# Reading wo in long runs inside the passes, and keeping four slabs of w1 in their buffers through one turn of a decode kernel

## The chip, the cores and the metric

One core of one Trainium2 chip. Times are device microseconds of one execution. Unless said otherwise a number "before" or "after" for a whole kernel is the median of several executions, and a number from inside a kernel is from the one execution that was profiled.

## The reference, cut to what matters

Two layers of attention for one new token over a cache of 65536 positions, each followed by a dense part with squared ReLU; the same caches and weights serve both layers. The function returns the result and the gradients of all inputs.

```python
def _A_ref(x, k_cache, v_cache, wq, wo):        # 32 query heads, 4 kv heads, 65536 positions, 128 wide
    q = (x @ wq) ...                            # wq 1024 x 4096
    p = softmax(q @ k * 128 ** -0.5)
    return (p @ v).reshape(1, 1, 4096) @ wo     # wo 4096 x 1024
def _B_ref(x, w1, b1, w2, b2):                  # w1 1024 x 3584, w2 3584 x 1024
    h = x @ w1 + b1
    return relu(h) ** 2 @ w2 + b2
x = x + _A_ref(ln(x), ...); x = x + _B_ref(ln(x), ...)
x = x + _A_ref(ln(x), ...); x = x + _B_ref(ln(x), ...)
# outputs: x, and jax.vjp of it at grad_out: dx, dK, dV, dwq, dwo, dw1, db1, dw2, db2; all bf16
```

## The kernel before

The kernel runs four passes over the caches: two forward ones, then two backward ones. Between two passes lies a "turn" with the dense parts. Everything large goes through one arena of slots of 8 KB per partition. In a pass, the rest of the work (the products with wq and wo, and in the fourth pass the weight gradients) is cut into steps by Python generators, and the pipeline takes at most one background step per item.

How a weight is cut into slabs, and how wo and w1 are read:

```python
def slabs(name, load, nk, kper, ncols, ahead=1, flat=False):
    def fetch():                       # two adjoining slots if there are any: one load of 2 MB; else 1 MB each
        ...
        if ks and flat and NOW["wide"] and not odd_one():
            i = take_pair()
        ...
        nc.sync.dma_start(out=v, in_=load(k, kn))
def wo_slabs(g, ahead=1):
    v = A_wo.rearrange("(kc p) n -> p kc n", p=P)      # a partition's piece of a row block: 2048 bytes
    return slabs("s_wo", lambda k, kn: v[:, g * R + k:g * R + k + kn, :], R, 4, 1024, ahead, True)
def w1_slabs(ahead=1):
    v = rows_of(B_w1)                                  # 7168 bytes per partition and slab, eight slabs
    return slabs("s_w1", lambda k, kn: v[:, k:k + kn, :], DC, 1, F, ahead)
```

The product with wo in a forward pass (`g_wo`) and the one that gives dO in a backward pass (`g_dO`), with the end of the latter:

```python
def g_wo(L, xacc, g, ps=ps_bg, it=None):
    def fin(p):
        nc.vector.tensor_tensor(out=xacc[:], in0=xacc[:], in1=p, op=ALU.add)
    yield from g_mv(it or wo_slabs(g)[0], R, 8, lambda kc: L["oTb"][:, g * R + kc:g * R + kc + 1], ps, fin)

def dO_finish(L, g):
    def fin(y):
        ...                 # two DVE operations
        yield
        ...                 # one matmul
        yield
        ...                 # five small DVE operations
    return fin

def g_dO(L, dx, g):         # reads wo_slabs(g), multiplies each slab by dx broadcast, sums on ACT into y, then fin(y)
    yield from g_rowdots(wo_slabs(g)[0], R, dx[:], DC, dO_finish(L, g), "%s_dO%d" % (L["name"], g))
```

What an item of the pipeline does in the background. `urgent` holds the products of a head group, `normal` the weight gradients:

```python
class Background:
    def step(self, i):
        while self.later and i >= self.later[0][0]:
            self.add(*self.later.popleft()[1:])
        while self.urgent:
            r = next(self.urgent[0][1], "end")
            if r == "end":
                self.urgent.popleft()
                continue
            if r == "wait":
                break
            return
        while self.normal and self.done < self.total * i / self.steps:
            if next(self.normal[0], "end") == "end":
                self.normal.popleft()
            else:
                self.done += 1
                return
# fourth pass: 256 items plus 7 of lag; bg.steps = len(ITEMS[3]) - 4 = 252; bg.total = 150
```

The turn between the second and the third pass, where w1 is read twice, once for the forward product of layer 4 and once for its gradient:

```python
rows.add(w1_slabs()[0], DC, FC, lambda: dh4[:], fin_dx3, cols=f_cols, mix=True)     # second product
rows.add(wo_slabs(firstg[2])[0], R, DC, lambda: dx3[:], dO_finish(L3, firstg[2]), inplace=True)
run(g_w1(L4, ps_mv, pre=rows.fill))                                                 # first product
nc.vector.scalar_tensor_tensor(out=dh4[:], in0=dg4[:], scalar=2.0, in1=L4["r"][:], op0=ALU.mult, op1=ALU.mult)
rows.run()
```

## Time and profile before

| | before |
|---|---|
| median of three runs | 2010.06 us (2008.94 to 2014.95) |
| profiled run | 2017.21 us, clock 0.898, its span 2015.4 us |
| PE, DVE, ACT busy | 80%, 58%, 52% |
| moved | 794.97 MB in 110845 packets, mean 394 GB/s |
| last copy of scores in pass 1; in pass 2 | 351.3; 736.0 us |
| layer norm of the turn done; last ds of pass 3 | 766.2; 1148.4 us |
| first, 57th and last (64th) X of pass 4 | 1219.4; 1902.9; 1980.2 us |
| end | 2015.4 us |

The last rows are marks that I read off the records of single instructions. "ds" is the gradient of the scores in the third pass (32 of them), "dx3" the gradient that the turn hands to the third pass, and "X" the DVE product of the gradient of the probabilities (in ps_sc) and the kept exponentials E in the fourth pass, one for every four items, 64 in all. The profiled run was 2 to 8 us slower than the three others, so differences of a few microseconds between single traces are not to be trusted. The lines of the profile that carry the argument stand in the prediction.

### The profile page before, as it was taken

To read this page: it belongs to the slowest core of one execution; us is meant where nothing else is said; L and a number is where in the kernel's file an instruction comes from. 1 tells how busy PE (TensorE), PEld (TensorE's weight loads), DVE (VectorE), ACT (ScalarE), POOL (GpSimd) and SP (SyncE) were. 2 spreads that over 40 slices of the span, in tenths; PEclk is the share of its full clock that TensorE was granted. 3 is DMA by queue.
4 is the path that set the end of the run, shared out by engine and by line. 5 is a ranking of instruction groups with operands and counts; after the bars stand their busy time and mean duration, and the time that the engine had idled before them with its cause. 6 is when DMAs were issued, how large, how long until landed. Compare 5 with 4: busy or idle time off the path is not lost. (4 is left out here: it accounts for less than half of the span.)

```text
span 2015.4 us, 67001 instructions
## 1 busy us (share of the span) xinstructions
PE 1613.8 (80%) x30210; PEld 1315.4 (65%) x30210; DVE 1175.3 (58%) x2358; ACT 1043.6 (52%) x1613; POOL 144.4 (7%) x332
## 2 busy tenths in 40 slices
PE   6877787687887787868787888788778988698896
PEld 6877777677777686767777785455445555455554
DVE  5655455255555544535454476586658777577675
ACT  3444344253443353426354365586657677577675
POOL 0000000000000000000000001121111111121111
PEclk9999899699899997999888998799879889798888
DMA  9999999999999998999999986999999999999995
GB/s 389 420 419 420 419 422 399 391 406 419 420 417 419 420 404 316 371 420 420 418 413 417 394 305 254 363 404 424 421 405 404 408 419 399 358 405 424 416 377 236
DMA packets 110845, 794.97 MB, mean 394 GB/s; under 512 B 9424, under 2 KB 9438, under 8 KB 49374
## 3 DMA queue, kind: packets, MB, share of 16 engines
q1 hardware_dynamic: 86510, 624.99, 76.3%
q0 software_dynamic: 24048, 165.70, 19.9%
q8 instruction: 236, 3.87, 0.8%
q14 instruction: 51, 0.42, 0.1%
HBM read 624.96 MB, written 165.69 MB: 392 GB/s over the span
## 5 line engine op out<-in xcount | busy, mean ns | idle before, releaser
L153 DVE COPY kt<-ps_tr 128x1024 bf16<-128x1024 bf16 x724 | 497.7, 689 | 481.3 <-PE ps_tr L936 255.4
L150 ACT CAST arena<-ps_gg 128x1024 bf16<-128x1024 f32 x452 | 440.0, 1010 | 226.0 <-PE ps_gg L1303 169.7
L936 PE MATMUL ps_tr<-ident_b,arena 128*128 128x128 bf16 x3840 | 311.3, 226 | 55.7 <-DMA arena<-in_A_k_cache_dram 41.4
L936 PEld LDWEIGHTS <-arena 128*128 128x128 bf16 x3840 | 235.2, 101 | 62.3 <-DMA arena<-in_A_k_cache_dram 44.4
L153 DVE CAST arena<-ps_gg 128x1024 bf16<-128x1024 f32 (+1 forms) x191 | 228.9, 1199 | 77.3 <-PE ps_gg L1303 43.6
L150 ACT COPY kt<-ps_tr 128x1024 bf16<-128x1024 bf16 x164 | 172.3, 1055 | 185.9 <-PE ps_tr L1128 125.7
L1303 PE MATMUL ps_gg<-GG,xt 64*128 64x512 bf16 x1024 | 214.1, 417 | 46.3 <-DVE arena L153 26.1
L1038 PE MATMUL ps_acc<-arena 128*128 128x64 bf16 (+4 forms) x4096 | 204.7, 195 | 49.4 <-DMA arena<-in_A_v_cache_dram 28.9
L1249 PE MATMUL ps_tr<-ident_b,arena 128*128 128x128 bf16 x1824 | 178.2, 236 | 39.7 <-DMA arena<-in_A_v_cache_dram 38.8
L954 PE MATMUL ps_sc<-L_qpad,kt 128*128 128x64 bf16 (+7 forms) x3584 | 183.9, 194 | 19.6 <-issue 12.3
L1019 ACT ACTIVATE arena<-S_sb,L_negm 128x128 bf16<-128x128 f32 x256 | 165.7, 1003 | 58.2 <-DVE L_negm L1004 58.2
L1128 PE MATMUL ps_tr<-ident_b,arena 128*128 128x128 bf16 x1920 | 155.8, 227 | 46.5 <-DMA arena<-in_A_v_cache_dram 45.2
L1038 PEld LDWEIGHTS <-arena 128*128 128x128 bf16 x4096 | 158.5, 100 | 52.6 <-DMA arena<-in_A_v_cache_dram 32.9
L1249 PEld LDWEIGHTS <-arena 128*128 128x128 bf16 x1824 | 121.1, 105 | 94.3 <-issue 51.0
L954 PEld LDWEIGHTS <-kt 128*128 128x128 bf16 x3584 | 153.7, 100 | 25.7 <-issue 15.3
L1128 PEld LDWEIGHTS <-arena 128*128 128x128 bf16 x1920 | 118.1, 102 | 50.0 <-DMA arena<-in_A_v_cache_dram 47.9
L1329 PE MATMUL ps_acc<-X,arena 128*128 128x64 bf16 (+3 forms) x2048 | 120.7, 199 | 23.0 <-DMA arena<-in_A_k_cache_dram 23.0
L1019 ACT ACTIVATION_READ_ACCUMULATOR arena<-S_sb,L_negm 128x1 f32 x256 | 128.0, 500 | 0.0
L1329 PEld LDWEIGHTS <-arena 128*128 128x128 bf16 x2048 | 87.8, 102 | 59.4 <-issue 34.2
L1303 PEld LDWEIGHTS <-xt 64*128 64x128 bf16 x1024 | 61.2, 94 | 86.7 <-issue 48.0
L1282 PE MATMUL ps_sc<-DOB,kt 128*128 128x64 bf16 (+3 forms) x1824 | 117.7, 200 | 0.0
L1173 PE MATMUL ps_acc<-dsT,arena 128*128 128x64 bf16 (+7 forms) x2048 | 104.0, 195 | 16.7 <-DMA arena<-in_A_k_cache_dram 12.2
(269 smaller groups left out, 2129.1 us busy)
## 6 DMA issues: line engine op xcount, KB each, us to landing
arena<-in_A_k_cache_dram SPq DMA_DIRECT2D x86, 2048.0 KB, 21.4
arena<-in_A_v_cache_dram SPq DMA_DIRECT2D x83, 2048.0 KB, 21.7
out_dram<-arena POOLq DMA_DIRECT2D x151, 1024.0 KB, 11.4
arena<-in_A_v_cache_dram SPq DMA_DIRECT2D x76, 1024.0 KB, 16.2
arena<-in_A_k_cache_dram SPq DMA_DIRECT2D x76, 1024.0 KB, 14.6
arena<-in_B_w_dram SPq DMA_DIRECT2D x32, 896.0 KB, 5.9
arena<-in_A_wq_dram SPq DMA_DIRECT2D x22, 1024.0 KB, 14.3
arena<-in_A_wo_dram SPq DMA_DIRECT2D x18, 1024.0 KB, 18.5
```

The costliest lines, as they stand in the source:

```text
L150: nc.scalar.copy(out=out, in_=in_)
L153: nc.vector.tensor_copy(out=out, in_=in_)
L936: nc.tensor.transpose(pt[:, i, :], kb8[:, i, :], ident_b[:, :])
L954: nc.tensor.matmul(state["ps_s"][:, s:s + w, :].rearrange("p a b -> p (a b)"), lhsT=kt[:, i, :], rhs=L["qpad"][:, g, 0:w, :].rearrange("p ...
L1019: nc.scalar.activation(out=E(p, g, c0, SU)[:, :, h], in_=S[:, h, :], func=ACTF.Exp, bias=L["negm"][:, g, su, h:h + 1], scale=SCALE, accum_ ...
L1038: nc.tensor.matmul(ps_o[:, 0:w, :], lhsT=vb8[:, i, :], rhs=E(p, g, c, w), start=(c % SU == 0), stop=(c % SU == SU - 1), skip_group_check=True)
L1128: nc.tensor.transpose(pt[:, i, :], vb8[:, i, :], ident_b[:, :])
L1173: nc.tensor.matmul(ps_dq[:, 0:w, :].rearrange("p a b -> p (a b)"), lhsT=kb8[:, i, :], rhs=dsT[:, s:s + w, :].rearrange("p a b -> p (a b)") ...
L1249: nc.tensor.transpose(pt[:, i, :], vb8[:, i, :], ident_b[:, :])
L1282: nc.tensor.matmul(state["ps_dp"][:, s:s + w, :].rearrange("p a b -> p (a b)"), lhsT=vt[:, i, :], rhs=DOB[:, g, 0:w, :].rearrange("p a b - ...
L1303: nc.tensor.matmul(pg[:, 512 * h:512 * h + 512], lhsT=xt[64 * h:64 * h + 64, j1 // 8 + m, :], rhs=gg[64 * h:64 * h + 64, :, :].rearrange(" ...
L1329: nc.tensor.matmul(ps_dq[:, 0:w, :].rearrange("p a b -> p (a b)"), lhsT=kb8[:, i, :], rhs=X[:, s:s + w, :].rearrange("p a b -> p (a b)"), ...
```

## The change

Two intents. First, the twelve groups of wo that are read inside passes are read with eight adjoining rows per partition: 16 KB in one piece if two adjoining slots are free, else twice 8 KB, where the kernel before has pieces of 2 KB. A partition then holds other rows than before, so o is rearranged by one matmul with a 0/1 matrix before the product, and dO is rearranged back after it. Second, in the turn the first product with w1 reads slabs 4 to 7, then 0 to 3, and leaves the last four in their slots for the second product. To make room for the new constants, some small tiles shrink and the bias rows move into an arena slot.

```diff
+    def wo_runs(g):
+        v = A_wo[g * 1024:(g + 1) * 1024, :].rearrange("(p k) n -> p k n", k=8)
+        return slabs("s_wo", lambda k, kn: v[:, k:k + kn, :], R, 4, 1024, 1, True)[0]
 ...
+    def w1_twice(keep):
 ...
+        def first():
+            for k in list(range(keep, DC)) + list(range(keep)):
+                sl, w = one(k)                    # takes a slot, issues the load
+                yield k, w
+                if k < keep:
+                    kept.append((sl, w))
+                else:
+                    sl.free()
+        def again():
+            for k in range(DC):
+                sl, w = kept[k] if k < keep else one(k)
+                NOW["slab"] = sl
+                yield k, w
+                sl.free()
 ...
     def g_wo(L, xacc, g, ps=ps_bg, it=None):
 ...
+        each = ...; yield                         # one DVE operation
+        pt = ...;   yield                         # one matmul with to_runs
+        own = ...; oruns = ...; orunb = ...; yield   # three DVE operations
+        yield from g_mv(wo_runs(g), R, 8, lambda kc: orunb[:, kc:kc + 1], ps, fin)
 ...
     def g_dO(L, dx, g):
-        yield from g_rowdots(wo_slabs(g)[0], R, dx[:], DC, dO_finish(L, g), "%s_dO%d" % (L["name"], g))
+        def fin(y):
+            each = tmp.tile([P, R, 8], F32, name="run_own", bufs=1)
+            nc.vector.tensor_tensor(out=each[:, :, :], in0=y.unsqueeze(1).to_broadcast([P, R, 8]),
+                                    in1=M8[:, :].unsqueeze(2).to_broadcast([P, R, 8]), op=ALU.mult)
+            yield
+            pt = ps_mv([P, R, 8], F32)
+            nc.tensor.matmul(...)                 # with from_runs
+            yield
+            own = ...; back = ...                 # two DVE operations
+            yield
+            yield from dO_finish(L, g)(back[:, :])
+        yield from g_rowdots(wo_runs(g), R, dx[:], DC, fin, "%s_dO%d" % (L["name"], g))
 ...
+    w1a, w1b = w1_twice(4)
-    rows.add(w1_slabs()[0], DC, FC, lambda: dh4[:], fin_dx3, cols=f_cols, mix=True)
+    rows.add(w1b, DC, FC, lambda: dh4[:], fin_dx3, cols=f_cols, mix=True)
-    run(g_w1(L4, ps_mv, pre=rows.fill))
+    run(g_w1(L4, ps_mv, pre=rows.fill, it=w1a))
```

Cut: five constants, the bias rows in a slot (`rows_f`), `gmb` in one buffer, `ndt4` as 64 x 16 broadcast in the matmul, and in `g_mv` a counter for the last slab, since the slabs now come in another order.

More of the change, by code (lines that the diff above doesn't have):

```diff
@@ L126 @@
     nc.vector.tensor_tensor(out=M4x[:], in0=M8[:, 0:4], in1=M8[:, 4:8], op=ALU.add)
+    eighth = const.tile([P, 8], F32, name="eighth")
+    nc.vector.tensor_reduce(out=eighth[:], in_=ident_f[:].rearrange("p (m e) -> p e m", e=8), axis=AX.X, op=ALU.add)
+    sixt = const.tile([P, 16], F32, name="sixt")
+    nc.vector.tensor_reduce(out=sixt[:], in_=ident_f[:].rearrange("p (m e) -> p m e", e=8), axis=AX.X, op=ALU.add)
+    to_runs = const.tile([P, 8, 16], BF, name="to_runs")
+    nc.vector.tensor_copy(out=to_runs[:, :, :], in_=sixt[:, :].unsqueeze(1).to_broadcast([P, 8, 16]))
+    sixt2 = const.tile([P, 16], F32, name="sixt2")
+    nc.vector.tensor_reduce(out=sixt2[:], in_=ident_f[:].rearrange("p (a m) -> p m a", m=16), axis=AX.X, op=ALU.add)
+    from_runs = const.tile([P, 16, 8], F32, name="from_runs")
+    nc.vector.tensor_copy(out=from_runs[:, :, :], in_=sixt2[:, :].unsqueeze(2).to_broadcast([P, 16, 8]))
     load = {"act": 0.0, "dve": 0.0, "pe": 0.0}
@@ L167, in col_from_dram_f @@
         nj = n // P
-        rows = tmp.tile([nj // 4, 4 * P], BF, name="rows_f", tag="rows_f", bufs=1)
-        nc.sync.dma_start(out=rows[:], in_=v1d.rearrange("(s x) -> s x", x=4 * P))
+        sl = Slot("rows_f")
+        rows = sl.t[0:nj // 4, 0:4 * P]
+        nc.sync.dma_start(out=rows, in_=v1d.rearrange("(s x) -> s x", x=4 * P))
         pt = ps_mv([P, 4, 8], BF)
@@ L178, in col_to_dram_f @@
         nj = n // P
-        rows = tmp.tile([nj // 4, P, 4], BF, name="rows_f", tag="rows_f", bufs=1)
+        sl = Slot("rows_f", True)
+        rows = sl.t[0:nj // 4, 0:4 * P].rearrange("s (p j) -> s p j", j=4)
         c3 = col[:, :].rearrange("p (s j) -> p s j", j=4)
@@ L184, in col_to_dram_f @@
             nc.vector.tensor_copy(out=rows[:, :, j], in_=pt[:])
-        nc.gpsimd.dma_start(out=v1d.rearrange("(s x) -> s x", x=4 * P), in_=rows[:].rearrange("s p j -> s (p j)"))
+        nc.gpsimd.dma_start(out=v1d.rearrange("(s x) -> s x", x=4 * P), in_=sl.t[0:nj // 4, 0:4 * P])
+        sl.free(stored=True)
     def col_to_dram(col, n, v1d):
@@ L460, in w1_slabs, with one @@
         return slabs("s_w1", lambda k, kn: v[:, k:k + kn, :], DC, 1, F, ahead)
+    def w1_twice(keep):
+        v = rows_of(B_w1)
+        kept = []
+        def one(k):
+            sl = Slot("s_w1")
+            w = sl.t[:, 0:F]
+            nc.sync.dma_start(out=w, in_=v[:, k, :])
+            return sl, w
+        def first():
[11 more added lines that the diff above has]
+                yield k, w
+                sl.free()
+        return first(), again()
     def w2_slabs(ahead=1):
@@ L470, in g_mv @@
         first = True
+        left = nk
         for kc, slab in slab_it:
+            left -= 1
             if ps_of is ps_bg and kc % 4 == 0:
@@ L475, in g_mv @@
             for nb in range(nbk):
-                last = (kc == nk - 1) and (nb == nbk - 1)
+                last = left == 0 and nb == nbk - 1
                 nc.tensor.matmul(ps[:, nb, :], lhsT=cols(slab, nb), rhs=xcol(kc).to_broadcast([P, rep]),
@@ L868, in fin @@
             nc.vector.tensor_tensor(out=xacc[:], in0=xacc[:], in1=p, op=ALU.add)
-        yield from g_mv(it or wo_slabs(g)[0], R, 8, lambda kc: L["oTb"][:, g * R + kc:g * R + kc + 1],
-                        ps, fin)
+        if it is not None:
+            yield from g_mv(it, R, 8, lambda kc: L["oTb"][:, g * R + kc:g * R + kc + 1], ps, fin)
+            return
+        each = tmp.tile([P, R, 8], BF, name="run_each", bufs=1)
+        nc.vector.tensor_tensor(out=each[:, :, :], in0=L["oTb"][:, gsl(g)].unsqueeze(2).to_broadcast([P, R, 8]),
+                                in1=eighth[:, :].unsqueeze(1).to_broadcast([P, R, 8]), op=ALU.mult)
+        yield
+        pt = ps_mv([P, R, 8])
+        nc.tensor.matmul(pt[:, :, :].rearrange("p r k -> p (r k)"), lhsT=to_runs[:, :, :].rearrange("p a b -> p (a b)"),
+                         rhs=each[:, :, :].rearrange("p r k -> p (r k)"), start=True, stop=True)
+        yield
+        own = tmp.tile([P, 8, R], F32, name="run_own", bufs=1)
+        nc.vector.tensor_tensor(out=own[:, :, :], in0=pt[:, :, :].rearrange("p r k -> p k r"),
+                                in1=M8[:, :].unsqueeze(1).to_broadcast([P, 8, R]), op=ALU.mult)
+        oruns = tmp.tile([P, 8], F32, name="run_o")
+        nc.vector.tensor_reduce(out=oruns[:], in_=own[:, :, :], axis=AX.X, op=ALU.add)
+        orunb = tmp.tile([P, 8], BF, name="run_ob")
+        nc.vector.tensor_copy(out=orunb[:], in_=oruns[:])
+        yield
+        yield from g_mv(wo_runs(g), R, 8, lambda kc: orunb[:, kc:kc + 1], ps, fin)
     def dO_finish(L, g):
@@ L892, in g_dO @@
     def g_dO(L, dx, g):
-        yield from g_rowdots(wo_slabs(g)[0], R, dx[:], DC, dO_finish(L, g), "%s_dO%d" % (L["name"], g))
+        def fin(y):
+            each = tmp.tile([P, R, 8], F32, name="run_own", bufs=1)
+            nc.vector.tensor_tensor(out=each[:, :, :], in0=y.unsqueeze(1).to_broadcast([P, R, 8]),
+                                    in1=M8[:, :].unsqueeze(2).to_broadcast([P, R, 8]), op=ALU.mult)
+            yield
+            pt = ps_mv([P, R, 8], F32)
+            nc.tensor.matmul(pt[:, :, :].rearrange("p r k -> p (r k)"), lhsT=from_runs[:, :, :].rearrange("p a b -> p (a b)"),
+                             rhs=each[:, :, :].rearrange("p r k -> p (r k)"), start=True, stop=True)
+            yield
+            own = tmp.tile([P, R, 8], F32, name="run_own", bufs=1)
+            nc.vector.tensor_tensor(out=own[:, :, :], in0=pt[:, :, :], in1=eighth[:, :].unsqueeze(1).to_broadcast([P, R, 8]), op=ALU.mult)
+            back = tmp.tile([P, R], F32, name="run_o")
+            nc.vector.tensor_reduce(out=back[:], in_=own[:, :, :], axis=AX.X, op=ALU.add)
+            yield
+            yield from dO_finish(L, g)(back[:, :])
+        yield from g_rowdots(wo_runs(g), R, dx[:], DC, fin, "%s_dO%d" % (L["name"], g))
     def dn_finish(dn, first):
@@ L995, in low @@
                 nc.vector.tensor_reduce(out=gm[:], in_=v["ptm"][:], axis=AX.X, op=ALU.min)
-                v["gmb"] = tmp.tile([R, P], F32, name="gmb")
+                v["gmb"] = tmp.tile([R, P], F32, name="gmb", bufs=1)
                 nc.vector.tensor_scalar(out=v["gmb"][:], in0=ones_f[0:R, :], scalar1=gm[:, 0:1], scalar2=None, op0=ALU.mult)
@@ L1215, in g_setup @@
                 nc.vector.tensor_tensor(out=CCf[:, g, 1, i * R:(i + 1) * R], in0=L["dOT"][:, sl], in1=L["rZ"][:, sl], op=ALU.mult)
-            ndt = dspool.tile([64, J, R2], BF, name="ndt4", tag="ndt4", bufs=1)
+            ndt = dspool.tile([64, R2], BF, name="ndt4", tag="ndt4")
             for i, L in enumerate((La, Lb)):
-                nc.vector.tensor_copy(out=ndt[:, :, i * R:(i + 1) * R], in_=L["nd2"][:, sl].unsqueeze(1).to_broadcast([64, J, R]))
+                nc.vector.tensor_copy(out=ndt[:, i * R:(i + 1) * R], in_=L["nd2"][:, sl])
             state["ndt"] = ndt
@@ L1279, in vS @@
                     nc.tensor.matmul(state["ps_dp"][:, :, :].rearrange("p c r -> p (c r)"), lhsT=sel2[:, :],
-                                     rhs=state["ndt"][:, :, :].rearrange("o c r -> o (c r)"), start=True, stop=False)
+                                     rhs=state["ndt"][:, :].unsqueeze(1).to_broadcast([64, J, R2]), start=True, stop=False)
                 w = min(4, J - s)
```

## The prediction

> **What bounds the kernel now.** I read the page's slices first, then the packet line and the issues by tensor, then 20 us stretches of the passes and 5 us stretches of the one dense turn that the change touches, then the instructions of that turn in order of time, and last the list of waits.
>
> ```profile
> DMA  9999999999999998999999986999999999999995
> GB/s 389 420 419 420 419 422 399 391 406 419 420 417 419 420 404 316 371 420 420 418 413 417 394 305 254 363 404 424 421 405 404 408 419 399 358 405 424 416 377 236
> DMA packets 110845, 794.97 MB, mean 394 GB/s; under 512 B 9424, under 2 KB 9438, under 8 KB 49374
> ...
> arena<-in_A_wo_dram SPq DMA_DIRECT2D x18, 1024.0 KB, 18.5
> arena<-in_A_wo_dram SPq DMA_DIRECT2D x7, 2048.0 KB, 19.6
> ```
>
> The digits say that the 16 DMA engines are busy nearly everywhere, at a plateau near 420 GB/s. Two dips lie in slices 15 (the turn between the second and third pass, 756 to 806 us) and 23 and 24 (the turn before the fourth pass). PE is 80% busy but not the bound: in the list of waits of the whole run, PE in the two forward passes waits 41.4 us for K and 28.9 us for V. So in the passes a microsecond of DMA time is a microsecond of the run; in a turn it need not be. The third line gives the packets: 49374 - 9438 = 39936 of 2 to 8 KB. By the code, wq and wo (four readings of each) are read as rows of 2048 bytes, 32768 packets; w1 (four readings) as 4096 packets of 7168 bytes; the rest are stores, 1024 of 7168 bytes and 2048 of 4096. The sum, 32768 + 4096 + 1024 + 2048, is 39936.
>
> What a short packet costs I took from the trace's records of single packets on the load queue, sorted by size: mean 88.9 ns for 2048 bytes, 303.9 ns for 7168, 327.0 for 8192, 621.5 for 16384. Sixteen KB in 2 KB pieces take 8 x 88.9 = 711 ns of an engine, in one piece 621.5, in two 654. The stretches agree:
>
> ```profile
> 100.00:120.00 20.00, 16.61 (x423) 15.91 (x421) 11.27 (x24) 9.22 (x24) 0.00 (x0) 1.00 1.02 418
> 120.00:140.00 20.00, 15.25 (x351) 14.68 (x348) 10.57 (x27) 7.07 (x17) 0.00 (x0) 0.91 1.02 415
> 160.00:180.00 20.00, 15.75 (x409) 15.32 (x408) 10.55 (x24) 9.10 (x22) 0.00 (x0) 1.00 1.01 425
> ```
>
> The columns after the engines are granted clock, DMA share, GB/s. A 2 MB group of wo was issued at 105.9 us and moved in the first two; they fall short of 425 by 7 and 10 GB/s, (7 + 10) x 20 us / 425 = 0.8 us of DMA time lost. By packets: 1024 x 88.9 / 16 = 5.69 us against 128 x 621.5 / 16 = 4.97 us, 0.72 us.
>
> The turn, on PE (start, duration, then in brackets the idle time before and what ended it):
>
> ```profile
> 766.55 4.81 PE L477 MATMUL ps_mv<-L_nb,arena 128*128 128x18 bf16 x140 [1.11 <-DVE L_nb L219]
> 772.64 1.11 PE L477 MATMUL ps_mv<-L_nb,arena 128*128 128x18 bf16 x28 [1.28 <-DMA arena<-in_B_w_dram]
> 775.21 1.11 PE L477 MATMUL ps_mv<-L_nb,arena 128*128 128x18 bf16 x28 [1.47 <-DMA arena<-in_B_w_dram]
> 777.40 1.10 PE L477 MATMUL ps_mv<-L_nb,arena 128*128 128x18 bf16 x28 [1.08 <-DMA arena<-in_B_w_dram]
> 779.41 0.37 PE L493 MATMUL ps_mv<-ident_f,dh 128*28 128x128 f32 x1 [0.90 <-DVE dh L1534]
> 780.38 1.89 PE L637 MATMUL ps_tr<-ident_b,arena 128*128 128x128 bf16 x16 [0.60 <-DMA arena<-in_B_w_dram]
> 782.07 1.48 PE L637 MATMUL ps_sc<-ident_b,arena 128*128 128x128 bf16 x12
> 783.35 1.27 PE L669 MATMUL ps_bg<-vcb,wt 128*128 128x64 bf16 x24
> ```
>
> Five slabs of w1 are there when the first product starts (5 x 28 matmuls at once); the sixth, seventh and eighth each arrive about 2.2 us apart and PE waits for each. Only then does the second product (L637 turns a slab, L669 multiplies) begin, and it waits for its own copy of slab 0. Twenty slots less eight held for E and seven for kept V blocks leave five, which is why three slabs come late.
>
> **What the Trainium skill says.** "DMA: Bandwidth & Descriptors", section "Why small descriptors are slow (HBM only)", gives each packet a fixed cost of about 3 cycles beside one cycle for 32 bytes. Estimated from it, 2048 bytes cost 67/64 and 16384 bytes 515/512, a gain of 4%. The trace has 711/621.5, 14%; I use the trace. The same page, section "Anatomy of one DMA — SWDGE (gpsimd) path", says that DMA engines do not wait on semaphores, the issuing sequencer does. The trace agrees for the SP queue: its own waits hold 547.5 us for stores that must leave a slot. A late slot thus delays every load behind it. "TensorE: Matmul & The Clock Gate", section "What's actually happening", says that an array seen idle runs at half clock. Here the granted clock was 0.50 from 770 to 780 us, and sixteen transposes took 1.89 us at 780.38 but 1.06 us at 784.47.
>
> **Part 1: wo in long runs.** Twelve groups of 2 MB are read inside passes (three in each); the four in the turns keep their 2 KB rows. I counted in the built program which get two adjoining slots: five are one load of 16 KB per partition, seven are two loads of 8 KB. Before: 12 x 1024 x 88.9 / 16 = 68.3 us. After: 5 x 128 x 621.5 / 16 = 24.9, plus 7 x 256 x 327.0 / 16 = 36.6; sum 61.5. Gain 6.8 us of DMA time. In the first three passes the share is 1.00 to 1.02 in nearly every stretch, so the nine groups there (five at 0.72 us and four at 5.69 - 5.23 = 0.46 us, 5.4 us) count in full. In the fourth it is mostly 0.9 to 1.02 with PE up to 99% busy, so of its 3 x 0.46 us I count half. Part 1: -6 us.
>
> **What it adds.** A forward group gets four small DVE operations and one matmul, a dO group three and one. At 0.2 us each (the 128x28 and 128x32 DVE operations of the trace take 0.18 to 0.19) that is 6 x 4 x 0.2 + 6 x 3 x 0.2 = 8.4 us of DVE, beside 1175 us. Each step is an item of the pipeline apart from the next (an item of the fourth pass is about 2.9 us, 775 us over 263), so nearly nothing waits; in the passes that DMA bounds it costs nothing. Five new constants at the start, some 1.5 us of DVE, lie beside the first loads. In the fourth pass the extra matmuls borrow a transpose buffer for one item, three times. The single ndt4 copy becomes smaller, which pays part of it. Sum: +0.5 us. The bias rows now use an arena slot; that shifts which slot each later load gets.
>
> **Part 2: four slabs kept.** The first product now reads slabs 4 to 7, then 0 to 3, which stay; the second reads only 4 to 7 again. That removes 4 x 128 packets of 7168 bytes, 3.67 MB, 512 x 303.9 / 16 = 9.7 us of DMA time. It is not worth 9.7 us: from 785 to 790 us the DMA moves 187 GB/s and waits for slots. What counts is the chain on PE, DVE and ACT. The three late slabs of the first product still use slots of the first three slabs, so the first product still ends at 778.5 us. But the order of the changed program puts 28, 20 and 8 transposes of the second product between the late slabs' matmuls: slabs 0 and 1 are already there, so the three waits of 1.28, 1.47 and 1.08 us are filled. The second product's multiplications can then start right after dh, near 779.6 us instead of 783.35: 3.7 us. DVE also waits 0.74 and 0.90 us for w1 late in that product; slabs 4 to 7 find their slots earlier now, so I add 0.8 us. Part 2: -4.5 us, and the third pass starts that much earlier.
>
> **Sum.** 2010 - 6 - 4.5 + 0.5 = 2000 us.
>
> **Rivals.** First: the turn gains nothing, because the second product is bound by turning and copying (26 pieces of 0.7 us after 785 us) and the five slots become tighter: four kept and one for the broadcast vector leave none until slab 0 is done. Against it, slab 0 is turned early in the new order, four slabs ahead of the need. It would leave 2004 us. Second: the fourth pass takes it back. It is in-order everywhere and has stalls that depend on which slot a load gets:
>
> ```profile
> DVE mv_t L553 <- DMA arena<-in_A_wo_dram: 16.7, 1, 16.7
> ```
>
> There DVE, and PE behind it, stood for 16.7 us for the second half of a wo group. By the slot counts of the two builds, the changed kernel fetches it at the same item with an equally old slot, so I expect this stall again; but the slots of other loads differ, and one more stall could cost 5 to 15 us (2006 to 2015), one less would give as much (1986 to 1995). Third: all removed DMA time counts, 6.8 + 9.7, which gives 1994 us; the idle stretches of the turn speak against it. Fourth: the SP queue, which stood 16.98 us on the load issued after the group of wo at 105.9 us, is freed and loads go out earlier. The engines were at 1.02 all that while, so I give it nothing.
>
> **Range and chances.** The known parts give 1994 to 2004; the three runs before lie within 6 us, and the fourth pass may move by 10 either way. I take 2000 us, 1989 to 2011 for 8 in 10. Two per cent is 40 us; neither part nor both can give or lose it: 1% faster, 98% within, 1% slower.
>
> **What would show it.** Packets under 8 KB should fall by 12288 + 512 to 36574, bytes to 791.3 MB, and packets in all to about 100,480 (2432 longer ones come). Stretches with wo should read near 424 GB/s instead of 415 to 418. In the turn, L637's transposes should stand between the last matmuls of the first product, and the time from the end of the first product to dx3 should shrink by 4 to 5 us. The prediction is wrong if the passes take as long with fewer packets (then DMA was not the bound), if PE waits for slabs 4 to 7, or if the fourth pass moves by more than 10 us.

## The result, and the profile after

| | before | after |
|---|---|---|
| median | 2010.85 us (4 runs, 2008.94 to 2014.95) | 2015.43 us (4 runs, 2010.95 to 2015.86) |
| ratio | | 1.0015, 95% interval 0.9994 to 1.0036: the same |
| profiled run | 2017.21 us | 2015.64 us, clock 0.903 |
| layer norm of the turn done | 766.2 | 762.4 |
| last ds of pass 3 | 1148.4 | 1145.4 |
| first, 57th, last X of pass 4 | 1219.4; 1902.9; 1980.2 | 1214.3; 1884.5; 1975.2 |
| end | 2015.4 | 2013.5 |

A ratio here is the mean time of one kernel's fast runs over that of the other's of the same rounds, so not quite the ratio of the medians. The class foretold ("within 2%") is right; the time is not: 2015.4 us lies above the range of 1989 to 2011, and 15 us above the 2000 predicted.

The traffic is what was predicted. Bandwidth by slice and packets, from the page of the changed kernel:

```profile
GB/s 389 421 424 420 423 424 404 392 396 420 425 420 424 425 393 272 346 421 423 419 423 411 391 325 254 360 425 423 411 381 424 420 423 423 312 423 424 423 339 224
DMA packets 100429, 791.30 MB, mean 393 GB/s; under 512 B 9376, under 2 KB 9390, under 8 KB 36526
```

36526 packets under 8 KB (36574 predicted), 791.3 MB as predicted. Slices 15 and 16, the turn, fell from 316 and 371 to 272 and 346 GB/s. That is some 3.5 MB less in the two (69 GB/s x 50.4 us), nearly the 3.67 MB that are no longer read: the time of the removed loads was left idle there, not filled with others. The stretches with the first group of wo, here with the long pieces (columns as in the prediction):

```profile
100.00:120.00 20.00, 15.55 (x364) 14.83 (x361) 9.60 (x21) 5.73 (x15) 0.00 (x0) 0.91 1.02 418
120.00:140.00 20.00, 16.51 (x397) 15.24 (x395) 11.52 (x33) 8.34 (x22) 0.00 (x0) 1.00 1.01 427
```

Before they had 418 and 415: the second rose as expected, the first did not.

PE in the turn of the changed kernel, in order of time (start, duration, line, and in brackets the idle time before):

```profile
762.70 4.81 PE L527 MATMUL ps_mv<-L_nb,arena 128*128 128x18 bf16 x140 [1.11 <-DVE L_nb L234]
767.37 1.87 PE L687 MATMUL ps_tr<-ident_b,arena 128*128 128x128 bf16 x16
769.03 1.49 PE L687 MATMUL ps_sc<-ident_b,arena 128*128 128x128 bf16 x12
770.31 1.11 PE L527 MATMUL ps_mv<-L_nb,arena 128*128 128x18 bf16 x28
771.27 1.16 PE L687 MATMUL ps_tr<-ident_b,arena 128*128 128x128 bf16 x16
772.27 0.39 PE L687 MATMUL ps_sc<-ident_b,arena 128*128 128x128 bf16 x4
772.50 1.06 PE L527 MATMUL ps_mv<-L_nb,arena 128*128 128x18 bf16 x28
773.41 0.61 PE L687 MATMUL ps_sc<-ident_b,arena 128*128 128x128 bf16 x8
775.61 1.10 PE L527 MATMUL ps_mv<-L_nb,arena 128*128 128x18 bf16 x28 [1.58 <-DMA arena<-in_B_w_dram]
777.61 0.27 PE L543 MATMUL ps_mv<-ident_f,dh 128*28 128x128 f32 x1 [0.91 <-DVE dh L1618]
777.79 0.47 PE L719 MATMUL ps_bg<-vcb,wt 128*128 128x64 bf16 x10
```

The transposes of the second product (L687) do stand between the last slabs' matmuls (L527), two of the three waits for slabs are gone, and the multiplications of the second product (L719) start 15.1 us after those of the first (777.79 - 762.70) where before it was 16.8 (783.35 - 766.55). That is 1.7 us, not the 3.7 predicted: the first product itself became longer, from 12.0 us (766.55 to 778.50) to 14.0 (762.70 to 776.71). And PE still waits for a slab of w1 that is read again, one of the signs of being wrong that the prediction named:

```profile
792.51 0.64 PE L687 MATMUL ps_sc<-ident_b,arena 128*128 128x128 bf16 x8 [1.48 <-DMA arena<-in_B_w_dram]
```

Now compare what the DMA engines do behind it. First the kernel before, then the changed one, 5 us each:

```profile
780.00:785.00 5.00, 4.62 (x62) 4.62 (x63) 1.48 (x3) 1.60 (x2) 0.00 (x0) 0.58 1.07 420
785.00:790.00 5.00, 5.00 (x86) 4.26 (x84) 4.10 (x7) 3.57 (x6) 0.00 (x0) 1.00 0.47 187
```

```profile
775.00:780.00 5.00, 3.49 (x60) 3.10 (x60) 2.32 (x11) 0.59 (x1) 0.00 (x0) 0.84 0.07 29
780.00:785.00 5.00, 5.00 (x57) 4.17 (x54) 3.47 (x6) 2.58 (x4) 0.00 (x0) 0.50 0.00 0
```

Ten microseconds with almost nothing moving. The load queue's own waits from 760 to 800 us say why:

```profile
SPq L490 <- PE ps_tr L687: 13.5, 2, 13.3
```

L490 is the load of a w1 slab in the changed kernel. It stood 13.3 us at a stretch until the transposes had read a kept slab and let its slot go. All loads behind it in the queue waited too.

And the end. The two rows of each kernel are the stretch from the 57th X to the end and that from the last X to the end; first before, then after:

```profile
1902.90:2015.40 112.50, 92.42 (x1142) 56.27 (x1140) 75.42 (x138) 70.73 (x78) 18.52 (x31) 0.85 0.80 316
1980.20:2015.40 35.20, 20.17 (x241) 11.24 (x239) 17.16 (x36) 14.54 (x17) 3.58 (x6) 0.72 0.45 181
```

```profile
1884.50:2013.50 129.00, 101.83 (x1184) 61.08 (x1181) 80.44 (x156) 75.49 (x83) 19.61 (x33) 0.79 0.77 312
1975.20:2013.50 38.30, 22.10 (x264) 12.47 (x259) 21.68 (x45) 19.77 (x23) 5.07 (x9) 0.78 0.56 220
```

The changed kernel reaches the 57th X 18.4 us earlier than the kernel before and ends only 1.9 us earlier. After that point it has 42 more PE instructions (1184 against 1142), 18 more on DVE, 5 more on ACT: work that the kernel before had done by then. So at least a part of the longer end is work in another place. (The granted clock is lower there as well, 0.79 against 0.85; see the open ends.)

Which work, the code tells. An urgent step that yields "wait" lets the item do a weight-gradient step as well; any other yield ends the item. The change puts three plain `yield`s into each dO group. I counted in the built programs of the fourth pass:

```
                     items that end in    weight-gradient   item (of 263) at which
                     an urgent step       steps             the last of them is done
before                     90                  150                252
after                      99                  150                261
```

Three groups of three pauses are nine items without a gradient step. The pass has 263 - 90 = 173 items for 150 steps, so the backlog is not made up before the tail. The third pass has nine such pauses too, but no gradient steps to lose. That was my theory after the result: **pacing**. Its rival, from the prediction, was that **slots** of later loads had shifted (the bias rows in the arena, the other order of loads), with a stall more in the fourth pass. Open besides was what the two intended parts were worth.

### The profile page after: what moved, and what is told of

Its sections match the earlier page's. It is cut to its first block, busy times and chain, and to the rows that moved or that the text cites. A ratio compares the mean times of both kernels' runs of the same rounds, so it can differ in the third digit from the quotient of the medians.

```text
span 2013.5 us, 67094 instructions
## 1 busy us (share of the span) xinstructions
PE 1610.2 (80%) x30228; PEld 1311.7 (65%) x30228; DVE 1177.5 (58%) x2409; ACT 1043.9 (52%) x1609; POOL 143.0 (7%) x332
## 2 busy tenths in 40 slices
DMA packets 100429, 791.30 MB, mean 393 GB/s; under 512 B 9376, under 2 KB 9390, under 8 KB 36526
## 5 line engine op out<-in xcount | busy, mean ns | idle before, releaser
L164 DVE CAST arena<-ps_gg 128x1024 bf16<-128x1024 f32 (+2 forms) x189 | 225.0, 1190 | 89.8 <-PE ps_gg L1386 43.6
L1037 PEld LDWEIGHTS <-kt 128*128 128x128 bf16 x3584 | 150.5, 99 | 19.3 <-ACT kt L161 9.8
L1256 PE MATMUL ps_acc<-dsT,arena 128*128 128x64 bf16 (+7 forms) x2048 | 103.4, 195 | 17.9 <-DMA arena<-in_A_k_cache_dram 12.7
L1365 PEld LDWEIGHTS <-kt 128*128 128x128 bf16 x1824 | 87.8, 104 | 42.7 <-issue 41.6
```

The source lines that it names most:

```text
L164: nc.vector.tensor_copy(out=out, in_=in_)
L1037: nc.tensor.matmul(state["ps_s"][:, s:s + w, :].rearrange("p a b -> p (a b)"), lhsT=kt[:, i, :], rhs=L["qpad"][:, g, 0:w, :].rearrange("p ...
L1256: nc.tensor.matmul(ps_dq[:, 0:w, :].rearrange("p a b -> p (a b)"), lhsT=kb8[:, i, :], rhs=dsT[:, s:s + w, :].rearrange("p a b -> p (a b)") ...
L1365: nc.tensor.matmul(state["ps_dp"][:, s:s + w, :].rearrange("p a b -> p (a b)"), lhsT=vt[:, i, :], rhs=DOB[:, g, 0:w, :].rearrange("p a b - ...
```

## The experiments

Each ran in five rounds beside the kernel before; all were correct except the one that is wrong. The four calls had medians of 2013.22, 2012.01, 2013.67 and 2012.29 us for the kernel before (11 runs each).

### The parts alone

**wo_only**: the changed kernel without the kept slabs.

```diff
-    w1a, w1b = w1_twice(4)
-    rows.add(w1b, DC, FC, lambda: dh4[:], fin_dx3, cols=f_cols, mix=True)
+    rows.add(w1_slabs()[0], DC, FC, lambda: dh4[:], fin_dx3, cols=f_cols, mix=True)
-    run(g_w1(L4, ps_mv, pre=rows.fill, it=w1a))
+    run(g_w1(L4, ps_mv, pre=rows.fill))
```

> The change without the w1 part: wo in 8 and 16 KB runs, the permutations, the bias rows in an arena slot. If the packet saving counts in the passes as predicted, the profile of the first three passes ends 5 us earlier than that of the kernel before (its first softmax-gradient and score copies by the same ordinal), and the time is 4 to 6 us shorter (ratio 0.997 to 0.998). Rival, the fourth pass gives it back: the third pass ends 5 us earlier but the time is within 2 us (ratio 0.999 to 1.001). Rival, the added slot and operations cost: the time is 3 us longer.

Measured: 2014.38 us, ratio 1.0006 (0.9993 to 1.0019); the third pass ends 2.7 us earlier (last ds at 1145.64 against 1148.37), not 5. Of the three forecasts the rival that the fourth pass gives it back comes nearest. **w1_only**: the kernel before with `w1_twice(4)` in the turn, the reverse of the edit above.

> The kernel before with only the four kept slabs of w1. By my prediction the turn is 4.5 us shorter and the third pass with it (ratio 0.998). Rival, from the two traces: the DMA queue stands idle for 9 us in the turn instead, because no slot is free, and the next pass resumes its stream no earlier; the third pass's later half is then within 1 us of before, and the ratio 0.999 to 1.001.

Measured: 2010.74 us, ratio 0.9994 (0.9981 to 1.0006), as its rival had it. Neither part alone gains or loses anything that can be told from zero. **rows_slot_only**: the kernel before with the bias rows in a slot.

```diff
-        rows = tmp.tile([nj // 4, 4 * P], BF, name="rows_f", tag="rows_f", bufs=1)
+        sl = Slot("rows_f")
+        rows = sl.t[0:nj // 4, 0:4 * P]
 ...        # and the same for the rows that are stored; sl.free() behind
```

> The kernel before with only the bias rows moved to an arena slot: no transfer is longer or shorter, only the slots that later loads get are shifted. If the shift of slots is what took the gain back, this alone is 3 to 6 us slower than before (ratio 1.0015 to 1.003). If not, it is within 2 us (0.999 to 1.001).

Measured: 2011.71 us, ratio 0.9990 (0.9978 to 1.0002). **after_own_rows**: the changed kernel with the bias rows in a tile of their own, the reverse edit.

> The changed kernel with the bias rows in a tile of their own again. If the slot took the gain back, this one has the predicted 2000 to 2005 us (ratio 0.995 to 0.9975). If the fourth pass takes it back for another reason, it has the changed kernel's time, ratio 1.000 to 1.002.

Measured: 2017.83 us (2009.57 to 2019.88), ratio 1.0013 (0.9995 to 1.0030), as the changed kernel. The shift of slots by the bias rows is not the cause, in either direction.

### The pacing

**pace_wait**: the changed kernel with its three new pauses in a dO group no longer counted as steps. An item with such a pause goes on to a gradient step, and no wait or dependence changes.

```diff
             nc.vector.tensor_tensor(out=each[:, :, :], ...)
-            yield
+            yield "wait"
             pt = ps_mv([P, R, 8], F32)
             nc.tensor.matmul(...)
-            yield
+            yield "wait"
 ...
-            yield
+            yield "wait"
             yield from dO_finish(L, g)(back[:, :])
```

> The changed kernel with one thing undone: the three new pauses of a dO group no longer take the turn of the weight gradients' background work. In the changed kernel each of them does, and by the programs' own count the background work ends at item 261 of 263 instead of 252. If those nine steps in the tail are what took the passes' gain back, this kernel is 4 to 8 us faster than the changed one (2007 to 2011 us, ratio to before 0.996 to 0.9985), and from the 57th X of the fourth pass to the end takes 113 us as in the kernel before instead of 124 to 129. Rival, the tail is long only because PE falls to half clock there by chance: the time stays at 2013 to 2015 us, ratio 1.000 to 1.0015.

Measured: 2003.69 us (2000.02 to 2009.98), ratio 0.9968 (0.9951 to 0.9985): within the ratios expected, faster than the microseconds expected. **before_lag**: the converse, the kernel before with three empty pauses in each dO group and nothing else.

```diff
     def g_dO(L, dx, g):
+        def fin(y):
+            for _ in range(3):
+                yield
+            yield from dO_finish(L, g)(y)
-        yield from g_rowdots(wo_slabs(g)[0], R, dx[:], DC, dO_finish(L, g), "%s_dO%d" % (L["name"], g))
+        yield from g_rowdots(wo_slabs(g)[0], R, dx[:], DC, fin, "%s_dO%d" % (L["name"], g))
```

> The kernel before with three empty pauses added to each dO group and nothing else: no operation and no transfer more. If the lag of nine background steps is the cause, this is 4 to 8 us slower than before (ratio 1.002 to 1.004) and its stretch from the 57th X to the end is 10 us longer. Rival (chance clock, or the slots of wo): ratio 0.999 to 1.001.

Measured: 2020.02 us, ratio 1.0046 (1.0034 to 1.0059). Nine pauses that do nothing cost 0.0046, as much as undoing the pauses of the changed kernel gained (0.0047), and a little more than expected. The same two rows, from the 57th and from the last X to the end, of pace_wait and then of before_lag:

```profile
1890.90:2003.80 112.90, 91.11 (x1142) 55.58 (x1140) 75.72 (x138) 70.65 (x78) 18.49 (x31) 0.87 0.79 310
1969.00:2003.80 34.80, 19.33 (x241) 11.04 (x239) 17.17 (x36) 14.54 (x17) 3.58 (x6) 0.76 0.46 183
```

```profile
1893.90:2020.80 126.90, 101.92 (x1185) 61.04 (x1184) 80.52 (x157) 75.86 (x83) 19.74 (x33) 0.80 0.80 321
1982.50:2020.80 38.30, 22.20 (x264) 12.51 (x260) 21.70 (x45) 19.79 (x23) 5.09 (x9) 0.77 0.56 220
```

The instruction counts settle it: pace_wait has the 1142, 138 and 78 of the kernel before, before_lag the 1184 or so, 157 and 83 of the changed one. In the built programs the last gradient step falls at item 252 in pace_wait and at 261 in before_lag.

If work left for the end is dear, doing it earlier should pay. **after_both** is pace_wait in which an item of the fourth pass may do an urgent and a gradient step, and **before_both** the kernel before with the same; the last gradient step falls at item 235.

```diff
-                if r == "wait":
+                if r == "wait" or PS["pass4"]:
                     break
 ...
-    bg.steps = len(ITEMS[3]) - 4
+    bg.steps = len(ITEMS[3]) - 20
```

> The changed kernel in which, in the fourth pass, an item does an urgent step and a background step, and the background work is paced to end at item 235. If the end is set by the work left for the tail, the tail is shorter still, some 20 us less than the changed kernel's, and the time is 2000 to 2008 us. Rival, the middle of the fourth pass is bound by DMA and stores moved there lengthen it by as much: the time is that of the kernel with the pauses undone.

> The kernel before with the same pacing. If the tail is what binds, it gains 3 to 8 us too (ratio 0.996 to 0.9985), and the wo part shows as the difference between this kernel and the changed one with the same pacing: about 5 us in favour of the latter. Rival: ratio 0.999 to 1.001.

Measured: 2022.59 us, ratio 1.0062 (1.0048 to 1.0076), and 2026.15 us, ratio 1.0079 (1.0064 to 1.0093). My expectations for both failed outright. From the first to the 57th X after_both took 689.4 us (679.4 in pace_wait), and the tail did not shrink (115.8 us from the 57th X to the end, 112.9 in pace_wait). **pace_early** is the milder form: pace_wait with the gradients spread over fewer items, the last step at item 249.

```diff
-    bg.steps = len(ITEMS[3]) - 4
+    bg.steps = len(ITEMS[3]) - 36
```

> pace_wait with the background work spread over 32 items fewer of the fourth pass, so that it ends at item 249 of 263 and not at 252. If the work left for the tail sets the end: 1 to 2 us faster than pace_wait (ratio 0.996), with fewer PE and DVE instructions after the last X. If the fourth pass as a whole is full (as the runs with one more step in an item suggest, 10 us longer), it is the same or up to 3 us slower, the middle of the pass (33rd X) later by as much as the end gains.

Measured: 2011.67 us (2005.01 to 2018.37), ratio 0.9994 (0.9971 to 1.0016). The tail is 1.4 us shorter (111.5 us), the pass before it 10 us longer (689.4 us). By the ratios it loses 0.0026 against pace_wait, about 5 us, with an interval from nearly 0 to 11; the 3 us that I allowed for are not excluded. So of the paces tried that of the kernel before is the best: later loses at the end, earlier, as far as these runs show, within the pass. Why earlier costs as much as 10 us is not settled by these runs.

### What the two parts are worth when the pacing is right

**wo_pace**: pace_wait without the kept slabs (the edit of wo_only).

> pace_wait (the changed kernel with the three new pauses of a dO group not counted as steps; ratio 0.9968) without the four kept slabs of w1. It isolates what the kept slabs are worth when the pacing is repaired. If the turn's 2 to 3 us are carried to the end: 2006 to 2007 us, ratio 0.998, with the fourth ds of the third pass 3 to 6 us later than in pace_wait (838.6). If the DMA engines, idle for longer in the turn by as much as the loads removed, give nothing that lasts: 2003 to 2005 us, ratio within 0.001 of pace_wait's, and the last ds of the third pass within 1 us of pace_wait's 1141.9.

Measured: 2007.72 us, ratio 0.9968 (0.9955 to 0.9981). That is pace_wait's ratio. Three pairs differ in the four kept slabs alone: pace_wait against wo_pace 0.0000, w1_only against before -0.0006, after against wo_only +0.0009. The mean is 0.0001, with an interval that I estimate from theirs at 0.0012 either way (2.4 us): no gain to be seen, and not the 4.5 us predicted. One thing went against the forecast: the last ds of the third pass came at 1145.6 us, 3.7 later than in pace_wait and not within 1 us, so in these two traces the kept slabs did shorten the third pass, and the fourth did not pass it on. **long_only**: the kernel before with the long pieces and nothing else; no rearrangement, so a wrong result (relative error 1.23).

```diff
-        yield from g_mv(it or wo_slabs(g)[0], R, 8, ...
+        yield from g_mv(it or wo_runs(g), R, 8, ...
 ...
-        yield from g_rowdots(wo_slabs(g)[0], R, ...
+        yield from g_rowdots(wo_runs(g), R, ...
```

> The kernel before with the twelve groups of wo of the passes read in runs of 8 or 16 KB, and nothing else: no rearranged o and dO, so no added operation and no added pause (a WRONG RESULT on purpose: the rows of wo meet the wrong elements of o). It isolates the packets. If 6 us of DMA time were well counted: 2005 to 2007 us, ratio 0.997 to 0.998, last ds of the third pass 4 to 6 us before the 1148.4 of the kernel before, and 113 us from the 57th X to the end as in it. If the time removed is hidden in the passes: ratio 1.000, third pass as before.

Measured: 2009.72 us (2003.59 to 2014.00), ratio 0.9979 (0.9962 to 0.9996), 4.2 us of 2013 (1 to 8 by the interval). The last ds of the third pass is only 1.5 us earlier than in the kernel before, where I expected 4 to 6. With the 0.9990 of the bias rows' slot (0.9978 to 1.0002, so perhaps nothing) the product is 0.9969, near the 0.9968 of wo_pace: the added DVE operations and matmuls have no cost of their own that shows beside intervals of 0.0012 to 0.0017 either way.

### How many slabs to keep

**pace_keep2**: pace_wait with `w1_twice(2)`.

> pace_wait with two slabs of w1 kept in place of four (1.84 MB less read than in the kernel before in place of 3.67). If the kept slabs starve the loads behind them of slots, two leave two more slots: DMA idle in the 90 us after the layer norm falls from 15.7 us to about 12, slabs are not awaited by PE, and the turn's chain is as short as in pace_wait (dx3 at 36 to 38.6 us) or 1 us shorter; the end within 2 us of pace_wait's. If what counts are the bytes removed, it loses half of the gain: dx3 at 38 to 40 us.

Measured: 2003.04 us (2000.50 to 2005.96), ratio 0.9949 (0.9936 to 0.9962), the lowest of all. Half the bytes saved, and more gained: 0.0019 less than wo_pace in the same rounds. Its idle DMA time in the 90 us fell to 7.0 us where I expected about 12. Why two should beat four was open. **pace_keep1** and **pace_keep3** are the same with 1 and 3; **after_keep2** is the changed kernel with 2 and its pauses left as they are.

```diff
-    w1a, w1b = w1_twice(4)
+    w1a, w1b = w1_twice(2)
```

> pace_wait with one slab of w1 kept. If held slots are what costs: no idle DMA time beyond the kernel with none kept (8 to 10 us in the 90 us after the layer norm), the fourth ds of the third pass 2 to 3 us earlier after the layer norm than the 78.4 us of wo_pace, the end 2004 to 2006 us, ratio 0.9955 to 0.9968. If the two-slab build is only lucky in its slots: anything, with no order by the number kept.

> pace_wait with three slabs of w1 kept. If held slots are what costs: idle DMA time between the 7.0 us of two kept and the 15.7 of four, about 10 to 12, the fourth ds 73 to 76 us after the layer norm, ratio 0.995 to 0.997. If the two-slab build is only lucky in its slots: no such order.

> The changed kernel with two slabs kept in place of four, its pauses left as they are. If pacing and slots are separate and add up: pace_keep2's 0.9949 plus the 0.0038 to 0.0047 that the pauses cost in three other pairs, 0.9987 to 0.9996 (2010 to 2012 us), about 125 us from the 57th X to the end and 264 PE instructions after the last X. If the gain of two slabs is a matter of luck with slots downstream, it comes out as the changed kernel, 1.001 to 1.002.

Measured: pace_keep1 2005.83 us, ratio 0.9967 (0.9954 to 0.9981); pace_keep3 2004.99 us, 0.9955 (0.9937 to 0.9972); after_keep2 2009.26 us, 0.9984 (0.9967 to 1.0001). My expectation for the fourth ds of the third pass failed for both: 78.9 us with one kept and 78.4 with three, no better than with none. So did the one for the idle DMA time: 11.4 and 13.0 us, where 8 to 10 and 10 to 12 were expected. By the last ds of that pass there is a gain. The traces of all seventeen kernels, grouped by the number kept (means over the kernels of a group; times from the end of the layer norm in the turn; "idle" is 90 us less the busy share of the DMA engines, from the records of single packets):

| slabs kept | kernels | dx3 | last ds of pass 3 | DMA idle in 90 us | DMA time of the loads saved | saved less added idle | last ds against none |
|---|---|---|---|---|---|---|---|
| 0 | 7 | 41.4 | 383.0 | 9.3 | 0 | | |
| 1 | 1 | 39.3 | 380.5 | 11.4 | 2.4 | 0.3 | 2.4 earlier |
| 2 | 2 | 36.9 | 374.3 | 7.1 | 4.9 | 7.1 | 8.7 earlier |
| 3 | 1 | 37.8 | 380.4 | 13.0 | 7.3 | 3.6 | 2.6 earlier |
| 4 | 6 | 38.1 | 381.5 | 17.1 | 9.7 | 1.9 | 1.5 earlier |

The loads saved are kept slabs x 128 packets x 303.9 ns / 16. The two last columns go together within about 2 us: with two and with four kept slabs what the third pass gets from the turn is nearer to the DMA time saved less the DMA time left idle (7.1 and 1.9 against 8.7 and 1.5 us) than to the shortening of the chain to dx3 (4.5 and 3.3). With one kept slab it is the other way round (0.3 and 2.1 against 2.4). From two to four kept slabs the idle time grows as the theory of held slots says; that it is longer with one slab than with two or with none is not explained, and for one and three there is a single trace each. So the rival in the expectations, that two slabs are only lucky in which slots they get, is not ruled out: after_keep2 shows that the gain comes again with other pauses, but its turn is the same. The same two stretches of the turn in pace_keep2 (5 us each, the last column GB/s) show the bubble nearly closed, against the 29 and 0 GB/s of the changed kernel:

```profile
775.00:780.00 5.00, 4.82 (x87) 4.42 (x86) 3.05 (x12) 2.97 (x4) 0.00 (x0) 0.82 0.93 350
780.00:785.00 5.00, 5.00 (x101) 4.54 (x98) 5.00 (x11) 3.72 (x6) 0.00 (x0) 1.00 0.29 74
```

## Why the prediction was wrong

The account that the runs give, in parts of the 2012 us or so of the kernel before: wo in long pieces with the bias rows' slot, -6.4 us (ratio 0.9968 of wo_pace); four kept slabs, 0 (three pairs, above); nine pauses, +8.4 us. The last is the mean of four pairs that differ in those pauses alone: after 1.0015 against pace_wait 0.9968, before_lag 1.0046 against 1, wo_only 1.0006 against wo_pace 0.9968, after_keep2 0.9984 against pace_keep2 0.9949; differences of 0.0047, 0.0046, 0.0038 and 0.0035, mean 0.0042. Each of these differences is clear of zero by the intervals of its two runs. The sum is +2 us; measured was 1.0015, +3.

1. **What bounds the kernel: right for the passes.** Fewer and longer packets made the kernel faster, in long_only with nothing else changed (0.9979, interval below 1).
2. **Part 1, -6 us: right within the noise.** It came out at 4.2 us (1 to 8) for the packets alone and 6.4 with what else came with them. In the traces, the layer norm of the turn, behind two of the three passes counted in full, is done at 762.7 us in the mean of twelve kernels with long pieces and at 766.8 in the mean of the five without: 4.1 us earlier.
3. **"What it adds", +0.5 us: this step failed.** It read "Each step is an item of the pipeline apart from the next ..., so nearly nothing waits". The first half is the very mechanism of the loss. I costed the operations and asked what they delay; I did not ask what an item with such a step does not do. The item gives up its gradient step, and the pass has no room to make nine of them up. From the traces of the fourth pass, the mean over the five kernels with these pauses (after, after_own_rows, wo_only, before_lag, after_keep2) against nine without them at the same pace (before, rows_slot_only, w1_only, wo_pace, long_only, pace_wait, pace_keep1 to 3): 672.5 against 678.4 us from the first to the 57th X, and 125.7 against 113.0 from there to the end. Nine steps give back 5.9 us where they are taken out, 0.7 us each, and cost 12.7 us at the end, 1.4 us each. Measured in place of +0.5: +8.4 us by ratios, +6.8 by these traces.
4. **Part 2, -4.5 us "and the third pass starts that much earlier": the chain was right in direction, the conclusion failed.** The chain to dx3 shrank by 3.3 us on average over the six kernels that keep four slabs (3.7 + 0.8 predicted), and by 1.7 in the changed kernel itself (39.3 against 41.0). "The first product still ends at 778.5 us" was wrong there: with the transposes between its matmuls it took 2 us longer. The 0.8 us did not come either: from 762 to 812 us DVE waited 2.3 us for slabs of w1, before 1.6. But the third pass is bound by DMA (a mean share of 1.00 from 830 to 1145 us in the changed kernel, 1.01 before), and its end moved by 1.5 us, not 4.5; by the time of the whole kernel nothing is left. I had seen that DMA stood idle at 785 to 790 us and took it as proof that saved loads were worth little; I should have counted how much more it would stand idle. "Slabs 4 to 7 find their slots earlier now" was wrong: one waited 13.3 us.
5. **The rivals.** The second ("the fourth pass takes it back") came nearest in outcome and in size (2006 to 2015), but was argued by slots and stalls, which rows_slot_only and after_own_rows rule out as far as the bias rows go: that it came near was luck. The stall of 16.7 us that I watched is there after the change as well, nearly as long, as expected, only with another victim. From the list of waits of the changed kernel (us in all, times, longest):

```profile
DVE X L1373 <- DMA arena<-in_A_wo_dram: 13.0, 1, 13.0
```

   The first rival (the turn gains nothing because the five slots get too tight) named the wait that point 4 found, and I argued it away by the order of PE's work alone. The third (all removed DMA time counts) fails with the 9.7 us of the kept slabs; the fourth (the load queue freed earlier) was not tested by itself.

What stays open: how much of the 1.4 us per step in the tail is the lower granted clock there (0.78 to 0.83 in the five kernels with the pauses, 0.85 to 0.88 in the nine without, from the 57th X on) and how much the lack of other work beside it; no run separates them. And why spreading the gradients over fewer items costs 10 us in the pass, and whether two kept slabs do well by their number or by the slots they happen to get.

The version to use is pace_keep2: 2003.04 us, 0.5% faster than the kernel before, with an interval (0.9936 to 0.9962) that excludes both kernels' ratios. It is ahead of four kept slabs in two pairs (pace_keep2 and pace_wait, after_keep2 and after: 0.0019 and 0.0031; mean 0.0025, by my estimate 0.0017 either way), while three kept (pace_keep3, 0.9955) cannot be told from two by the time.

## What to carry to other kernels

Where a scheduler gives each item of a pipeline one background step, a new pause is not free because little work stands in it: count the items that it takes from the rest of the background work, and look where that work ends. Where the stage after is bound by DMA, judge a saved load by what the queue does meanwhile: time saved less time newly idle because the kept buffer holds up the loads behind; here two kept slabs beat four. When a stage reaches a mark earlier and the end does not move, compare the instruction counts after the mark before looking for stalls.

## What the Trainium skill lacked or had wrong

- "DMA: Bandwidth & Descriptors", section "Why small descriptors are slow (HBM only)": its fixed cost per packet gives an estimate of 4% more time for 2048-byte than for 16384-byte packets. The records of the kernel before show 14% by the mean packet (8 x 88.9 against 621.5 ns), and 5% for two of 8192 bytes (2 x 327.0); long_only shows that the whole kernel gains by it, 4.2 us.
- "TensorE: Matmul & The Clock Gate", section "What's actually happening": it lets about 3.4 us of sustained work end the half clock. In the changed kernel PE is busy in the profile for 10 us of 10 at a granted clock of 0.50 (82 matmuls, whose ends the profile models; weight loads are busy 5.33 us). So in this stretch, busy as the profile gives it did not end the half clock. With the columns as before:

```profile
1955.00:1965.00 10.00, 10.00 (x82) 5.33 (x80) 4.86 (x6) 5.29 (x6) 1.88 (x3) 0.50 0.61 246
```

- "Perfetto Trace Analysis", section "Optimization Strategies": it sets as the goal to keep the matmul engine as busy as possible. In the turn, filling PE's waits with transposes shortened the chain to dx3 by 3.3 us and moved the end of the next pass by 1.5; the idle DMA time, up from 9.3 to 17.1 us, told more. Its section "Optimization Strategy" speaks of interleaving stages, but not of where the interleaved work ends: nine steps done nine items later cost 8.4 us.
- No page that I read has the cost of holding a buffer for reuse when loads share one in-order queue: the 13.3 us that one load waited for a kept slab's slot.
